# Written order for two engines only in the gate/up stage, and transform-D operands made as in the other blocks, in a Fourier-mixing and SwiGLU kernel on one Trainium2 core

## The chip, the cores and the metric

The kernel runs on one core of one Trainium2 chip, in float32. Its metric is the time of one execution in device microseconds. The engines of a core work side by side, each in the order of its own instruction queue: TensorE (PE; PEld is its weight load), ScalarE (ACT), VectorE (DVE), GpSimd (POOL) and SyncE (SP). SyncE issues nearly all transfers; GpSimd issues some, among them those that add to what lies in the destination (accumulating transfers).

## The reference

With x of 2048 x 512, w1 and w3 of 512 x 1376, w2 of 1376 x 512 and the real and imaginary parts of two discrete Fourier transforms:

```python
g = sigmoid((x * gate_w).sum(-1, keepdims=True))
a = x @ dft_hid_re.T
b = x @ dft_hid_im.T
y = dft_seq_re @ a - dft_seq_im @ b
h = silu(x @ w1) * (x @ w3)
out = g * y + (1 - g) * (h @ w2)
```

## The kernel before

**Products.** Each matrix product is done on 2 x 2 blocks with seven products instead of eight. Their operands are the blocks B11, B21 and B22 and the sums T1 = B12 + B11, T2 = T1 + B22, T3 = B22 + B12 and T4 = T2 + B21 (signs are put into the inputs on the host). Every operand is cut into a high and a low part: `split` (lines 110 and 111) makes the high part with a ScalarE copy and the low part with a VectorE subtraction. `mm3` (line 115) then issues three matmuls, high x high, high x low and low x high, so all TensorE work has line 115. The forms of the stationary side ("a1" and "a2", seven in all) are made by `forms1` (four of them, 1 MB) and `forms2` (three, 0.75 MB).

**Stages.** (1) *gate/up*: 22 items, one for each of 11 chunks of 128 columns of w1 and w3 and each half g of the tokens, with the exception that item 0 is done in a plain way ahead of the loop. (2) *F*: the transform along S, four blocks of 512 rows of the result; it comes before the transform along D here, and its result, scaled by g, goes to `zsp` in DRAM. (3) *H*: h @ w2, two blocks, with h read back from `hsp` and the result, scaled by 1 - g, stored to `nbsp`. (4) *Y*: the transform along D of z, two blocks, to which the `nbsp` part is added before it goes to `out`.

**gate/up.** `gate_up(n)` issues, for TensorE: X (six matmuls with form 4 of wb) and Z of item n, the first product X of item n + 3 (form 0 of its wa), X and Z of item n, Y of item n + 3, the last X of item n. That makes 42 matmuls; the last three items have no item n + 3 and 30 matmuls. An item's chunk comes as `ws` (load on SyncE, line 197); `prep_wa` splits three of its forms into `wa` (four buffers), `prep_wb` makes four sums on VectorE (lines 217 to 220) and splits them into `wb` (two buffers). The second time a chunk is used, `wb` is loaded from `wbsp` (line 202). ScalarE copies the first X and Z out of PSUM (lines 285 and 287) before TensorE may add to them again, applies silu (252 and 297), and VectorE adds and multiplies (250, 290, 292, 293, 298). GpSimd stores h (line 276). `extra[n]` holds more work, written after item n's own: the operands of the second token half (`sum_xo`, `split_xo`), the forms of part of w2 (`prep_w2`) and of x as stationary side of stage F (`make_a`). `prep_wa` for item n + 3 is written at the start of `gate_up(n)`, thus behind the extras of item n - 1.

**Order.** What is issued outside a region of written order is put in order by a planner with a timing model of its own; inside a region, each engine that the region names issues its instructions as they are written. In the kernel before, one region for all engines starts at `gate_up(1)` and ends with the kernel. What precedes it (loads, item 0, the first products of items 1 to 3) is ordered by the planner.

**Stages F, H and Y** run through one list, `STEPS`. A block has seven products in an order (`ORDER`), each in NQ steps: 4 in F, 3 in H, 2 in Y. A step issues 12 matmuls (6 for the last part of some H operands). The blocks begin at steps 0, 28, 56, 84 (F), 112, 133 (H), 154 and 168 (Y); the list ends at 182. `step(m)` issues the matmuls, then `advance(m)`: `load_c` loads operands whose entry in `LOADS` lies up to eight steps ahead, as far as the 13 buffers of 512 KB in `F4` are free; `sum_c` makes the T sum of step m + 4 on VectorE (line 532); `split_c` splits the operand of step m + 3 into one of four `zo` buffers. In F and H, T3 is made in the buffer of B22: after B22's split, GpSimd issues an accumulating transfer of B12 into it (line 548). In Y, T1 and T3 have loads of their own: SyncE loads B12 (line 557) and GpSimd adds B11 or B22 with an accumulating transfer (line 559).

The chain's order is P1 (B11), P5 (T1), P6 (T2), P3 (B22), P7 (T3), P2 (B21), P4 (T4). P1, P5, P6 and P3 use the first four forms, the others the last three. Both Y blocks of the kernel before use P1, P2, P5, P6, P3, P7, P4.

`at(block, n, f)` has f issued ahead of step n of a block. `load_forms` (line 691, on SyncE) loads a pair p of forms of the D matrices from `dsp`: the first four forms of p (1 MB) into buffer a1_k, the last three (0.75 MB) into a2_k, with k = 6, 7, 0, 1 for p = 0 to 3. Stage H uses buffers 0 to 5. `spill` (lines 647 to 659) scales or adds a result and stores it from SyncE. `close` at the end of gate/up gives the memory of its pools to stages F to Y.

The sites of the change are in the text below with their lines.

Of the kernel before, what the change touches and what calls it, by code (L numbers as in the profile page):

```python
# [10 lines left out]
ALU = mybir.AluOpType  # L11
# [4 lines left out]
F = 1376  # L16
KD = D // P
TB = 512
NTB = S // TB
NT = TB // P  # L20
NST = S // P
NG = NST // 2
NC = (F + P - 1) // P
NP2 = (NC + 1) // 2
# [9 lines left out]
def fnet_swiglu_gate_kernel(  # L34
# [20 lines left out]
    nc = tc.nc  # L55

    def pool(name, bufs, side, space=None):
        kw = {} if space is None else {"space": space}
        cm = tc.tile_pool(name=name, bufs=bufs, side=side, reuse_waits="tile", **kw)
        return cm, cm.__enter__()  # L60
# [37 lines left out]
    def wide(name):  # L98
        return take(F4, [P, 1024], F32, name)

    def parts(name):
        return take(ZO, [P, 2, 4, 256], F32R, name)

    def free(*tiles):
        for t in tiles:
            _, places, at = HELD.pop(id(t))
            places.append(at)

    def split(hi, lo, src):
        nc.scalar.activation(hi, src, AF.Copy)  # L110
        nc.vector.tensor_sub(lo, src, hi.bitcast(F32))  # L111
# [10 lines left out]
    dsp = [dram.tile([KD, P, 2, n, 256], F32, tag=f"dsp{n}", name=f"dsp{n}") for n in (4, 3)]  # L122
# [340 lines left out]
    for p, n in enumerate(A1_AT):  # L463
        extra.setdefault(n - 1, []).append(lambda p=p: load_a(p))
        extra.setdefault(n, []).insert(0, lambda p=p: make_a(p))
    extra.setdefault(NI - 2, []).append(lambda: load_a(NG - 1))
    extra[NI - 1] = [lambda: load_c(2)]


# [5 lines left out]
    CHAIN = (("P1", "B11"), ("P5", "T1"), ("P6", "T2"), ("P3", "B22"),  # L475
             ("P7", "T3"), ("P2", "B21"), ("P4", "T4"))

    NB = NTB + 4
    KIND = "F" * NTB + "HHYY"
    ORDER = [CHAIN] * (NTB + 2) + [tuple(CHAIN[i] for i in (0, 5, 1, 2, 3, 4, 6))] * 2  # L480
    NQ = [{"F": NG // 2, "H": NP2 // 2, "Y": KD // 2}[k] for k in KIND]
    STEPS = [(blk, q, k, form) for blk, nq in enumerate(NQ) for k, form in ORDER[blk]
             for q in range(nq)]
    START = [sum(NQ[:blk]) * len(CHAIN) for blk in range(NB + 1)]

    NEED = {
# [3 lines left out]
    }  # L490
    PLACE = {k: {"T1": "B12", "T2": "B12", "T4": "B12", "T3": "B22"} for k in "FH"}
    PLACE["Y"] = {"T2": "T1", "T4": "T1"}

    DONE = {k: ({"T1": "B11", "T4": "B21"}, {"T4": "B12", "T3": "B22"}) for k in "FH"}
    DONE["Y"] = {"T4": "B21"}, {"B11": "B11", "T4": "T1", "B22": "B22", "T3": "T3"}
    LEAD = 3
    AHEAD = 5
    RESULT = {"P3": 2, "P7": 3, "P2": 0, "P4": 1}
    FORM = {"P1": 0, "P5": 1, "P6": 2, "P3": 3, "P2": 0, "P4": 1, "P7": 2}
    RAW, ZT = {}, {}  # L500
    LOADS = sorted((START[blk] + n * nq - e * (blk > 0 or n != 1) + q, blk, k, q)
                   for blk, nq in enumerate(NQ) for q in range(nq) for k, n, e in NEED[KIND[blk]])

    def z_rows(tb, k):
        return zsp[(tb * 4 + k) * P : (tb * 4 + k + 1) * P, :]

    def block(blk, k, q):
        if KIND[blk] == "F":
            return cc[blk, ("B11", "B12", "B22", "B21").index(k), q]
        if KIND[blk] == "H":  # L510
            return hsp[blk - NTB, ("B11", "B12", "B21", "B22").index(k), q]
        return z_rows(2 * (blk - NTB - 2) + (k in ("B12", "B22")), 2 * (k in ("B21", "B22")) + q)

    def cols(blk, q, form):

        return 512 if KIND[blk] == "H" and q == NQ[blk] - 1 and form in ("B21", "B22", "T4") else 1024

    def done(m, j):
        blk, q, k, form = STEPS[m]
        if form in DONE[KIND[blk]][j]:  # L520
            free(RAW.pop((blk, DONE[KIND[blk]][j][form], q)))

    def sum_c(m):

        if not 0 <= m < len(STEPS):
            return
        blk, q, k, form = STEPS[m]
        b = {"T1": "B11", "T2": "B22", "T4": "B21"}.get(form)
        if b and form in PLACE[KIND[blk]]:
            n = cols(blk, q, b)  # L530
            t = RAW[blk, PLACE[KIND[blk]][form], q][:, :n]
            nc.vector.tensor_add(t, t, RAW[blk, b, q][:, :n])  # L532
        done(m, 0)

    def split_c(m):

        if not 0 <= m < len(STEPS):
            return
        blk, q, k, form = STEPS[m]
        src = RAW[blk, PLACE[KIND[blk]].get(form, form), q]  # L540
        ZT[m] = parts(f"zo{m}")
        t = ZT[m].rearrange("p h a n -> p h (a n)")
        n = cols(blk, q, form)
        split(t[:, 0, :n], t[:, 1, :n], src[:, :n])
        if form == "B22" and KIND[blk] != "Y":
            if n < 1024:
                nc.gpsimd.memset(src[:, n:], 0.0)
            nc.gpsimd.dma_start(src, block(blk, "B12", q), accum_op=ALU.add)
        done(m, 1)

    def load_c(m):

        while LOADS and LOADS[0][0] <= m and F4:
            _, blk, k, q = LOADS.pop(0)
            r = RAW[blk, k, q] = wide(f"{k}_{blk}_{q}")
            n = cols(blk, q, k)
            nc.sync.dma_start(r[:, :n], block(blk, "B12" if k in ("T1", "T3") else k, q)[:, :n])
            if k in ("T1", "T3"):
                nc.gpsimd.dma_start(r, block(blk, "B11" if k == "T1" else "B22", q),
                                    accum_op=ALU.add)  # L560

    def advance(m):
        load_c(m + LEAD + AHEAD)
        sum_c(m + LEAD + 1)
        split_c(m + LEAD)

    ctx.enter_context(tc.manual_schedule())
    for n in range(1, NI):
        gate_up(n)
        if ITEMS[n] == (NC - 1, 1):  # L570
            close(xo0_cm)
            a1_cm, a1 = pool("a1", 1, "left")

    split_c(0)
    split_c(1)
    close(*gate_pools)
    zo_b_cm, zo_b = pool("zo_b", 1, "right")
# [181 lines left out]
    def at(blk, n, f, *a):  # L759
        todo.setdefault(START[blk] + n, []).append((f, a))  # L760
# [10 lines left out]
    for i, (src, sp, p) in enumerate(late):  # L771
        blk, n = 1 + i // 2, 1 + i % 2 * 10
# [7 lines left out]
        at(NTB, p + 1, load_forms, "H", 1, p, w2sp, p)  # L780
    nh = 3 * NQ[NTB]
    for p in range(KD):
        at(NTB + 2, p - nh, load_forms, "Y", 0, p, dsp, (NP2 + p) % NG)
        at(NTB + 2, (p - 6, -2)[p >= NG - NP2], load_forms, "Y", 1, p, dsp, (NP2 + p) % NG)
    for blk in (NTB + 2, NTB + 3):
        for i, (k, form) in enumerate(ORDER[blk]):
            if k in RESULT:
# [66 lines left out]
```

## Time and profile before

| | |
|---|---|
| three runs, median | 819.0 us (817.43 to 820.0) |
| profiled execution | 816.77 us, span 815.0 us, mean granted clock 0.958 |
| TensorE busy | 751.5 us (92%), 3089 matmuls |
| VectorE, ScalarE busy | 576.3 us (71%), 365.4 us (45%) |
| GpSimd busy | 55.8 us (7%) |
| HBM | 132.64 MB read, 57.16 MB written, 233 GB/s |
| stages by the start of their matmuls | gate/up 5.6 us (24.3 for the loop), F 289.8, H 608.5, Y 717.0 |

TensorE's busy time is modelled, and a busy matmul can be one at a lower granted clock, so the count of matmuls in a stretch says more than its busy share: in stages F and H, 20 us hold 87 to 89 matmuls (0.225 us each).

### The profile page before, as it was taken

The page shows a single profiled execution, that of the slowest core. Times are in us where ns is not written, and L with a number is a line of the kernel's source. Part 1 is how long each engine was busy: PE and PEld are TensorE (multiplying, and loading weights), DVE is VectorE, ACT ScalarE, POOL GpSimd, SP SyncE. Part 2 cuts the span into 40 slices and gives each one's busy share as a digit, 9 for nine tenths or more (in the row PEclk, how much of TensorE's full clock was granted, in tenths as well). Part 3 has the DMA queues.
Part 4 walks back from the last instruction along what each step waited for, and adds up shares of the span by engine and source line. Part 5 has one row for each costly group of instructions (what it writes and reads, how often), then busy time and mean ns, then how long its engine had stood idle before and what let it go on. Part 6 is the DMA issues. An engine that isn't in the chain of part 4 may idle for free.

```text
span 815.0 us, 8527 instructions
## 1 busy us (share of the span) xinstructions
PE 751.5 (92%) x3089; PEld 594.1 (73%) x3089; DVE 576.3 (71%) x711; ACT 365.4 (45%) x485; POOL 55.8 (7%) x80
## 2 busy tenths in 40 slices
PE   9999888977868789999999999999999999977998
PEld 6777657765646567878878887888778778855886
DVE  7877766544455579698769877985878595844875
ACT  6554444333233346554545454444535445423452
POOL 0111000110000100100010010001000001000000
PEclk9999999888879879999999999999999999997999
DMA  6675323566365594858495658765999696797982
GB/s 232 202 303 192 142 90 116 188 218 226 137 241 205 219 399 181 227 213 317 144 286 209 243 171 242 279 237 162 316 397 402 167 312 151 257 385 241 347 266 79
DMA packets 50778, 190.36 MB, mean 234 GB/s; under 512 B 5296, under 2 KB 5424, under 8 KB 46128
## 3 DMA queue, kind: packets, MB, share of 16 engines
q1 hardware_dynamic: 40016, 144.20, 48.3%
q0 software_dynamic: 10432, 45.10, 19.3%
q8 instruction: 24, 0.39, 0.2%
q10 hardware_dynamic: 288, 0.52, 0.2%
q14 instruction: 18, 0.15, 0.1%
HBM read 132.64 MB, written 57.16 MB: 233 GB/s over the span
## 4 chain that ended last, share of the span: by engine, by line
PE 47%; DVE 18%; DMA 13%; issue 12%; ACT 9%; SPq 1%; POOL 0%; ACTq 0%; POOLq 0%; DVEq 0%
PE P L115 31%; PE X L115 9%; DMA B<-cc 5%; PE Z L115 4%; DVE zo L111 4%; ACT zo L110 3%; DMA B<-zsp 2%; DMA Y<-dsp 2%; DMA xs<-xn 1%; PE C L115 1%; DVE s L250 1%; DVE B L532 1%; DVE wa L111 1%; DMA B<-hsp 1%; DVE h L292 1%
## 5 line engine op out<-in xcount | busy, mean ns | idle before, releaser
L115 PE MATMUL P<-zo,a 128*128 128x512 f32 x1344 | 314.9, 395 | 5.6 <-DVE zo L111 3.8
L115 PEld LDWEIGHTS P<-zo,a 128*128 128x128 f32 x1344 | 253.5, 189 | 67.0 <-DVE zo L111 7.7
L111 DVE TENSOR_TENSOR zo<-B,zo 128x1024 fp32r<-128x1024 f32 (+1 forms) x166 | 197.6, 1201 | 89.4 <-ACT zo L110 88.8
L110 ACT ACTIVATE zo<-B 128x1024 fp32r<-128x1024 f32 (+1 forms) x166 | 171.3, 1041 | 190.4 <-PE P L115 69.3
L115 PE MATMUL X<-xo,wb 128*128 128x512 f32 x378 | 105.3, 427 | 9.1 <-ACT h L285 8.2
L115 PE MATMUL P<-zo,H 128*128 128x512 f32 x468 | 108.2, 392 | 0.4 <-DVE zo L111 0.4
L115 PEld LDWEIGHTS P<-zo,H 128*128 128x128 f32 x468 | 87.7, 188 | 20.8 <-DVE zo L111 1.3
L115 PEld LDWEIGHTS X<-xo,wb 128*128 128x128 f32 x378 | 78.2, 209 | 30.5 <-ACT h L285 10.3
L115 PE MATMUL P<-zo,Y 128*128 128x512 f32 x336 | 82.4, 407 | 11.8 <-DMA Y<-dsp 11.5
L115 PEld LDWEIGHTS P<-zo,Y 128*128 128x128 f32 x336 | 65.4, 196 | 28.7 <-DMA Y<-dsp 6.8
L532 DVE TENSOR_TENSOR B<-B,B 128x1024 f32<-128x1024 f32 (+1 forms) x66 | 78.1, 1183 | 0.2 <-DMA B<-hsp 0.2
L115 PE MATMUL X<-xo,wa 128*128 128x512 f32 x126 | 43.5, 473 | 31.6 <-ACT wa L110 26.9
L115 PEld LDWEIGHTS X<-xo,wa 128*128 128x128 f32 x126 | 24.9, 215 | 45.7 <-ACT wa L110 30.7
L252 ACT ACTIVATE s<-s 128x512 f32<-128x512 f32 x21 | 13.3, 631 | 70.0 <-DVE s L250 70.0
L290 DVE TENSOR_TENSOR u<-u,X 128x512 f32<-128x512 f32 x21 | 14.4, 684 | 38.2 <-PE X L115 38.1
L115 PE MATMUL Z<-xo,wa 128*128 128x512 f32 x126 | 34.9, 415 | 0.0
L298 DVE TENSOR_TENSOR h<-h,u 128x512 f32<-128x512 f32 x21 | 14.5, 692 | 26.6 <-ACT h L297 26.6
L115 PE MATMUL Y<-xo,wa 128*128 128x512 f32 x126 | 32.6, 393 | 0.0
L115 PE MATMUL Z<-xo,wb 128*128 128x512 f32 x126 | 32.5, 392 | 0.0
L115 PEld LDWEIGHTS Z<-xo,wa 128*128 128x128 f32 x126 | 26.3, 208 | 6.6
L276 POOL DMA_DIRECT2D hsp<-h x22 | 16.2, 736 | 181.4 <-DVE h L298 137.8
L115 PEld LDWEIGHTS Y<-xo,wa 128*128 128x128 f32 x126 | 23.7, 188 | 5.5
(109 smaller groups left out, 591.0 us busy)
## 6 DMA issues: line engine op xcount, KB each, us to landing
B<-cc SPq DMA_DIRECT2D x64, 512.0 KB, 6.5
hsp<-h POOLq DMA_DIRECT2D x22, 512.0 KB, 4.2
B<-hsp SPq DMA_DIRECT2D x20, 512.0 KB, 8.8
wbsp<-wb POOLq DMA_DIRECT2D x8, 1024.0 KB, 5.9
wb<-wbsp SPq DMA_DIRECT2D x8, 1024.0 KB, 5.1
B<-cc POOLq DMA_DIRECT2D x16, 512.0 KB, 10.2
H<-w2sp SPq DMA_DIRECT2D x6, 1024.0 KB, 9.8
B<-zsp SPq DMA_DIRECT2D x12, 512.0 KB, 13.0
```

Of the source, the lines that this page charges most:

```text
L110: nc.scalar.activation(hi, src, AF.Copy)
L111: nc.vector.tensor_sub(lo, src, hi.bitcast(F32))
L115: nc.tensor.matmul(ps, u, v, start=first and n == 0, stop=last and n == 2, skip_group_check=chain)
L250: nc.vector.tensor_add(s1, s1, y)
L252: nc.scalar.activation(s1, s1, AF.Silu)
L276: nc.gpsimd.dma_start(o.rearrange("b p n -> p b n"), h.rearrange("p (b n) -> p b n", b=2))
L290: nc.vector.tensor_add(u4, u4, x)
L292: nc.vector.tensor_add(u2, u2, z)
L298: nc.vector.tensor_mul(g1, g1, u4)
L532: nc.vector.tensor_add(t, t, RAW[blk, b, q][:, :n])
```

## The change

Three things are changed; what is computed stays the same. First, the region of written order around the gate/up loop names only TensorE and SyncE, so ScalarE, VectorE and GpSimd are ordered by the planner there. After the loop a region for all engines begins, as before. Second, in stage Y the first block takes the chain's order and only the last keeps the other. T1 and T3 of Y have no loads of their own any more: T1 is B12 plus B11 by a VectorE add, T3 is B22 plus an accumulating transfer of B12 after B22's split, as in F and H. Third, the loads of D forms are placed anew: pairs 0 and 1 at 24 and 23 (first forms) and 21 and 20 (last forms) steps ahead of stage Y, which is from three steps ahead of the second H block on. Pairs 2 and 3 come 7 and 6 steps ahead (first forms, as before) and one step ahead of and at the first step (last forms). Before, the first forms came 9 to 6 steps ahead and the last ones 6, 5, 2 and 2.

```diff
-    ORDER = [CHAIN] * (NTB + 2) + [tuple(CHAIN[i] for i in (0, 5, 1, 2, 3, 4, 6))] * 2
+    ORDER = [CHAIN] * (NB - 1) + [tuple(CHAIN[i] for i in (0, 5, 1, 2, 3, 4, 6))]
...
-    NEED = {
-        "F": (("B11", 0, 0), ("B12", 1, 1), ("B22", 2, 1), ("B21", 5, 0)),
-        "H": (("B11", 0, 0), ("B12", 1, 1), ("B22", 2, 1), ("B21", 5, 0)),
-        "Y": (("B11", 0, 0), ("B21", 1, 0), ("T1", 2, 6), ("B22", 3, 1), ("T3", 5, 6)),
-    }
-    PLACE = {k: {"T1": "B12", "T2": "B12", "T4": "B12", "T3": "B22"} for k in "FH"}
-    PLACE["Y"] = {"T2": "T1", "T4": "T1"}
-
-    DONE = {k: ({"T1": "B11", "T4": "B21"}, {"T4": "B12", "T3": "B22"}) for k in "FH"}
-    DONE["Y"] = {"T4": "B21"}, {"B11": "B11", "T4": "T1", "B22": "B22", "T3": "T3"}
+    NEED = [(("B11", 0, 0), ("B12", 1, 1), ("B22", 2, 1), ("B21", 5, 0))] * (NB - 1)
+    NEED.append((("B11", 0, 0), ("B21", 1, 0), ("B12", 2, 1), ("B22", 3, 1)))
+    PLACE = {"T1": "B12", "T2": "B12", "T4": "B12", "T3": "B22"}
+
+    DONE = {"T1": "B11", "T4": "B21"}, {"T4": "B12", "T3": "B22"}
...
-        if form == "B22" and KIND[blk] != "Y":
+        if form == "B22":
             if n < 1024:
                 nc.gpsimd.memset(src[:, n:], 0.0)
             nc.gpsimd.dma_start(src, block(blk, "B12", q), accum_op=ALU.add)
...
-            nc.sync.dma_start(r[:, :n], block(blk, "B12" if k in ("T1", "T3") else k, q)[:, :n])
-            if k in ("T1", "T3"):
-                nc.gpsimd.dma_start(r, block(blk, "B11" if k == "T1" else "B22", q),
-                                    accum_op=ALU.add)
+            nc.sync.dma_start(r[:, :n], block(blk, k, q)[:, :n])
...
-    ctx.enter_context(tc.manual_schedule())
+    order = tc.manual_schedule(engines={mybir.EngineType.PE, mybir.EngineType.SP})
+    order.__enter__()
     for n in range(1, NI):
         gate_up(n)
         if ITEMS[n] == (NC - 1, 1):
             close(xo0_cm)
             a1_cm, a1 = pool("a1", 1, "left")
 
+    order.__exit__(None, None, None)
+    ctx.enter_context(tc.manual_schedule())
     split_c(0)
     split_c(1)
     close(*gate_pools)
...
     for p in range(KD):
-        at(NTB + 2, p - nh, load_forms, "Y", 0, p, dsp, (NP2 + p) % NG)
-        at(NTB + 2, (p - 6, -2)[p >= NG - NP2], load_forms, "Y", 1, p, dsp, (NP2 + p) % NG)
+        early = p < NG - NP2
+        at(NTB + 2, p - (24 if early else nh), load_forms, "Y", 0, p, dsp, (NP2 + p) % NG)
+        at(NTB + 2, p - (21 if early else 3), load_forms, "Y", 1, p, dsp, (NP2 + p) % NG)
```

The rest of the diff replaces look-ups by kind of block by the single tables above.

More of the change, by code (lines that the diff above doesn't have):

```diff
@@ L501, in fnet_swiglu_gate_kernel @@
     LOADS = sorted((START[blk] + n * nq - e * (blk > 0 or n != 1) + q, blk, k, q)
-                   for blk, nq in enumerate(NQ) for q in range(nq) for k, n, e in NEED[KIND[blk]])
+                   for blk, nq in enumerate(NQ) for q in range(nq) for k, n, e in NEED[blk])
     def z_rows(tb, k):
@@ L519, in done @@
         blk, q, k, form = STEPS[m]
-        if form in DONE[KIND[blk]][j]:
-            free(RAW.pop((blk, DONE[KIND[blk]][j][form], q)))
+        if form in DONE[j]:
+            free(RAW.pop((blk, DONE[j][form], q)))
     def sum_c(m):
@@ L528, in sum_c @@
         b = {"T1": "B11", "T2": "B22", "T4": "B21"}.get(form)
-        if b and form in PLACE[KIND[blk]]:
+        if b:
             n = cols(blk, q, b)
-            t = RAW[blk, PLACE[KIND[blk]][form], q][:, :n]
+            t = RAW[blk, PLACE[form], q][:, :n]
             nc.vector.tensor_add(t, t, RAW[blk, b, q][:, :n])
@@ L539, in split_c @@
         blk, q, k, form = STEPS[m]
-        src = RAW[blk, PLACE[KIND[blk]].get(form, form), q]
+        src = RAW[blk, PLACE.get(form, form), q]
         ZT[m] = parts(f"zo{m}")
```

## The prediction, made before the changed kernel was built or run

> **What bounds the kernel now.** I read the forty slices first. TensorE shows 9 in nearly all slices from 320 to 700 us; it falls off in slices 5 to 15 (about 100 to 310 us, gate/up) and in slice 36 (720 to 740 us, the start of the D transform). The time to be won lies there. Next, windows cut at the start of each gate/up item (time range, length, busy us of PE, PEld, DVE, ACT and POOL, granted clock, DMA share, GB/s), with one window at the D start:
>
> ```profile
> 45.93:55.73 9.80, 9.80 (x44) 7.90 (x43) 7.17 (x12) 4.60 (x7) 1.28 (x2) 1.00 0.73 293
> 136.57:153.05 16.48, 12.74 (x43) 9.57 (x42) 8.40 (x15) 5.51 (x10) 1.97 (x3) 0.79 0.54 199
> 180.17:194.18 14.01, 11.72 (x43) 8.89 (x42) 6.80 (x12) 4.62 (x8) 0.72 (x1) 0.88 0.51 178
> 136.57:286.33 149.76, 118.52 (x428) 90.66 (x427) 77.67 (x132) 51.74 (x91) 14.09 (x21) 0.85 0.56 202
> 717.00:741.00 24.00, 12.16 (x41) 8.37 (x39) 8.37 (x8) 7.22 (x8) 1.71 (x2) 0.79 1.04 381
> ```
>
> The same 42 matmuls take 9.80 us where nothing is missing and 14.0 to 16.5 us where chunk or token preparation stands between. No engine is full in the long ones: VectorE has 6.80 us of work in 14.01. So this is an order problem, not a load problem. The waits between 23 and 300 us name the instructions:
>
> ```profile
> ACT s L252 <- DVE s L250: 70.0, 18, 5.8
> PEld X L115 <- ACT wa L110: 30.7, 9, 7.5
> PEld X L115 <- DVE wa L111: 11.0, 15, 1.2
> PEld X L115 <- ACT h L285: 10.3, 5, 3.8
> ```
>
> The timeline of the item at 180.17 shows how it comes about:
>
> ```profile
> 184.67 0.84 ACT L110 ACTIVATE a<-xm 128x768 fp32r<-128x768 f32 x1 [2.04 <-DVE xm L141]
> ...
> 185.42 0.83 ACT L110 ACTIVATE wa<-ws 128x768 fp32r<-128x768 f32 x1
> ...
> 186.30 0.73 PE L115 MATMUL X<-xo,wa 128*128 128x512 f32 x2 [1.89 <-ACT wa L110]
> ...
> 187.43 1.55 PE L115 MATMUL X<-xo,wa 128*128 128x512 f32 x4 [0.39 <-DVE wa L111]
> ```
>
> The split of wa needs only a loaded ws and the wa buffer that the Z product of the item before released, but ScalarE has it written behind the last silu of that item (L297) and behind make_a, whose second copy stands 2.04 us for VectorE's xm. Earlier in the item ScalarE idled up to 5.8 us at L252 with nothing allowed ahead. After such a gap the clock falls too.
>
> **Gate/up, the order of ScalarE, VectorE and GpSimd.** No instruction is added or removed. What is to be won is the excess over undisturbed items. Eight items from 35.89 to 126.91 take 91.0 us against 8 x 9.80 = 78.4, excess 12.6; nine to 255.84 take 128.9 against 9 x 9.66 (the item at 126.91) = 86.9, excess 42.0; the last three, of 30 matmuls (30 x 0.228 = 6.85), take 30.5 against 20.5, excess 9.9. Sum **64.5 us**. With ScalarE free to choose, the wa copy (0.83) and subtraction (0.96) fit in the 24 matmuls (5.5 us) between the Z product that frees the buffer and the first product that needs it.
> A bad order of the planner's is bounded by rows: 0 left over if every item runs like that at 45.93, and half, 32 us, if late splits remain in every second item. I take 0.65 us for each of 20 items, 13 us: the items at 55.73 and 66.29 took 10.56 and 10.61, 0.8 over, with a single 1.05 us xo split ahead of wa, at clock 1.00. The planner's own order can be read only ahead of gate_up(1): TensorE is busy 18.81 of the first 20 us with VectorE and ScalarE at 14. That speaks for the low half. **Gain 52 (32 to 64).**
> Cover for it: VectorE has 148 us of work between 35.89 and 286.33, and 186 would be left. DMA: 202 GB/s x 149.8 us = 30.2 MB in 98 us (8 x 9.66 + 20.5) is 309 GB/s, under the 381 of the last window above. SyncE's queue keeps its order, so loads start as soon as before relative to TensorE.
> What a gap costs beyond itself: the item at 180.17 waits 1.89 + 0.39 us and is 4.35 over 9.66, so 2.1 more went to the clock (0.88). The Trainium skill (TensorE: Matmul & The Clock Gate, "HAM oscillation — how this bites in real kernels") puts the danger at TensorE gaps over some 3.4 us. The trace here loses clock at 2.3 us. If ten such gaps stayed, the rule would price them at 10 x 2.3 = 23 us, the row at 10 x 4.35 = 43.
>
> **Gate/up to transform along S.** From 288.2 to 312.2 TensorE issues 73 matmuls (73 x 0.2247 = 16.4, from 89 in 20 us) in 24 us: 7.6 lost to the two first splits behind the last silu, and to an xs load that lands in 12 us at DMA share 0.99. The second region is written in full as before; only the splits may slip ahead of the last gate/up work. Bounds 0 and 6; I take **2**.
>
> **The D start, T1 and T3, early forms.** Between 717.0 and 750.2 TensorE issues some 72 matmuls, 16.2 us of work, in 33.2: **17 us lost**. The DMA engines are full from 701 to 741 (share 1.0, about 365 GB/s, 14.6 MB), and Y<-dsp has the last word:
>
> ```profile
> PE P L115 <- DMA Y<-dsp: 11.5, 3, 5.8
> ```
>
> Four edits empty this burst. (a) Two pairs of forms, 2 x (1 + 0.75) = 3.5 MB, leave it for the start of the second w2 h block (640 to 660 us: 171 GB/s, share 0.56). There they stand in SyncE's queue beside the B<-hsp loads, which lead their use by 8 steps, some 21 us; 3.5 MB at 365 GB/s is 10 us, so it is covered, and would cost up to 5 us without that lead. (b) T1 drops its accumulating transfer for a VectorE add: 4 x 1.22 us in all; VectorE is at 44.5 of 64 us after 751, hidden. T3 drops the second read of a block: both together save 2 MB per block. So 14.6 - 5.5 = 9.1 MB, 25 us, with the first steps' share in front. (c) The first Y block takes the chain's order: its second forms are needed at step 8 instead of step 2, some 16 us later. (d) T3 is now B22 plus an accumulating DMA that GpSimd can issue only after B22's split, two steps ahead of T3's. The w2 h block shows the price of the chain:
>
> ```profile
> 680.49 1.05 ACT L110 ACTIVATE zo<-B 128x1024 fp32r<-128x1024 f32 x1
> 681.57 1.23 DVE L111 TENSOR_TENSOR zo<-B,zo 128x1024 fp32r<-128x1024 f32 x1 [1.98 <-ACT zo L110]
> ...
> 683.20 0.85 POOL L548 DMA_DIRECT2D B<-hsp  x1 [49.66 <-DVE zo L111]
> ...
> 691.37 1.06 ACT L110 ACTIVATE zo<-B 128x1024 fp32r<-128x1024 f32 x1 [1.60 <-DMA B<-hsp]
> 692.46 1.23 DVE L111 TENSOR_TENSOR zo<-B,zo 128x1024 fp32r<-128x1024 f32 x1 [1.44 <-ACT zo L110]
> ```
>
> From the start of B22's split to the end of T3's it takes 13.2 us (680.49 to 693.69), for the second of the pair 14.3 (682.76 to 697.03). In Y there are five steps of 12 matmuls in between (three of lead, two between the forms): 13.5 us. So it just misses, by 0 to 1 us a block; landings of up to 12 instead of 8.2 us would make that 4. Queued behind T3's split on ScalarE are the next block's splits. I take 1 us a block, 2 in all (0 to 8), and 1 (0 to 5) for what is left of the start: **gain 14 (4 to 17).**
>
> **Sum:** 816.8 (profiled execution, span 815.0) - 52 - 2 - 14 = 748.8. The profiled execution lies 2.2 under the median of the three runs, so I forecast **751**. All best bounds give 732, all worst 783.
>
> **Rivals.**
> *Half of gate/up only*, 18%: the planner's view of when things are ready is not the chip's, and in every second item a wa split or an L285 copy comes late; or the compressed stage meets a DMA limit (30.2 MB at 250 GB/s is 121 us instead of 98, 23 us back). For it: wb loads land in 5.1 us at 170 to 250 GB/s and have one item, 9.6 us, to do so. Against it: the item at 35.89 ran at share 1.00 and 357 GB/s in 10.04 us. With some 29 of gate/up's us gained instead of 52: 751 + 23, about 774.
> *Gate/up unchanged*, 5%: the planner keeps emission order on the free engines, so the change does not do there what it says. Only the D start pays: 819 - 14 = 805. Against it: ahead of gate_up(1), where the planner orders all, two X matmuls of item 1 stand at 15.40 between C matmuls of item 0.
> *Slower*, 11%: the planner puts consumers of loads (wa from ws, a from xr) at the head of ScalarE's queue as if data were there at once. The real landings are 4.2 to 6.3 us for ws and 5.5 for xr; ScalarE would stand with L285 behind it, whose slack is the 12 matmuls (2.7 us) of Z and X less its own 0.6. A stand of 5.5 us is then a gap of 3.4, with the clock's 2 us 5.4 an item, 20 x 5.4 = 108 against today's 64.5: 819 + 43 - 16 = 846. It turns slower from 4.0 us of loss an item ((64.5 + 16) / 20). Against it: in the planner's stretch of before, ScalarE's waits for loads are 0.2 to 1.4 us each.
>
> **Numbers.** The forecast, 66%, has its own range 731 to 770. The range 728 to 795 adds the half gain and leaves out the unchanged gate/up, the slower case and a tail. Within 0.3% (2.5 us, about what a measurement of this kernel can tell from no change) gets 1%; faster 88%, slower 11%.
>
> **What would show it.** Right: items of 9.6 to 10.5 us with clock 1.00 between 36 and the start of P; PEld X <- ACT wa under 5 us in total; first P matmul near 237 us; the first Y step without a wait for Y<-dsp; T3 splits waiting some us on an accumulate while TensorE loses under 2. Wrong: ScalarE waiting for ws or xr with L285 behind it; waits of X for wb<-wbsp; a TensorE gap ahead of P7 in Y.

## The result and the profile after

| | before | after |
|---|---|---|
| median | 818.89 us (817.43 to 820.0, 4 runs) | 753.57 us (752.89 to 756.34, 4 runs) |
| profiled execution | 816.77 us, span 815.0 us | 754.2 us, span 752.4 us |
| mean granted clock | 0.958 | 0.993 |
| last matmul of gate/up ends | 288.2 | 233.6 |
| first matmul of F | 289.83 | 236.47 |
| first matmul of Y | 717.0 | 664.61 |
| from there to the end | 98.0 us | 87.8 us |

The ratio of the times is 0.921, with a 95% interval of 0.9181 to 0.9238: 65 us less. The last four rows say where. By the end of gate/up 54.6 us are won; 1.2 of them go before the first matmul of F and 1.0 during F and H; Y gives 10.2 more. Together 62.6, the difference of the two spans.

The head of the page of the changed kernel, with its forty slices:

```profile
span 752.4 us, 8533 instructions
PE 726.2 (97%) x3089; PEld 580.0 (77%) x3089; DVE 574.7 (76%) x715; ACT 367.0 (49%) x485; POOL 52.4 (7%) x76
...
PE   9999999989897899999999999999999999999996
...
PEclk9999999999999999999999999999999999999999
...
HBM read 128.45 MB, written 57.16 MB: 247 GB/s over the span
```

TensorE now has a 9 almost everywhere. The same 3089 matmuls take 726.2 us of modelled time instead of 751.5; the clock falls much less in gate/up (0.99 granted from 23 to 240 us). HBM reads are 4.19 MB fewer, the 2 MB that each Y block no longer reads a second time.

Windows cut at the starts of gate/up items, as before (time range, length, busy us of PE, PEld, DVE, ACT and POOL, granted clock, DMA share, GB/s):

```profile
145.12:156.43 11.31, 9.69 (x44) 7.70 (x42) 4.71 (x9) 4.24 (x7) 1.27 (x2) 1.00 0.61 221
185.91:195.43 9.52, 9.52 (x44) 7.88 (x42) 7.87 (x15) 3.96 (x8) 1.97 (x3) 1.00 0.87 285
195.43:209.54 14.11, 11.41 (x43) 8.98 (x42) 7.25 (x14) 4.88 (x9) 0.74 (x1) 0.88 0.67 272
```

Most items are like the one at 185.91: 9.52 us with TensorE busy throughout. Three of the 17 with 42 matmuls after 35.79 us stand out, with 11.43 us (at 45.99), 11.31 (at 145.12) and 14.11 (at 195.43). The waits of the loop, 23 to 240 us (engine, line, what it waited for: us in all, times, longest):

```profile
ACT s L252 <- DVE s L250: 20.1, 13, 4.6
...
DVE xm L139 <- DMA gs<-sc: 5.7, 1, 5.7
ACT wa L110 <- DMA ws<-w: 5.7, 1, 5.7
ACT zo L110 <- issue: 5.7, 1, 5.7
...
PEld X L115 <- DVE u L290: 4.5, 3, 2.0
...
PEld X L115 <- ACT h L297: 3.3, 2, 3.1
...
PEld X L115 <- DVE wa L111: 1.2, 1, 1.2
```

X no longer waits for wa copies (30.7 us before, none now), and its waits for wa subtractions fell from 11.0 to 1.2. In their place stand three waits of 5.7 us each, on ScalarE and VectorE. One of them in the timeline of ScalarE:

```profile
192.30 0.59 ACT L242 ACTIVATE s<-X 128x512 f32<-128x512 f32 x1
198.60 0.85 ACT L110 ACTIVATE wa<-ws 128x768 fp32r<-128x768 f32 x1 [5.71 <-DMA ws<-w]
200.90 0.42 ACT L110 ACTIVATE a<-xr 128x256 fp32r<-128x256 f32 x1 [1.45 <-DMA xr<-xn]
201.22 0.61 ACT L252 ACTIVATE s<-s 128x512 f32<-128x512 f32 x1
201.74 0.58 ACT L297 ACTIVATE h<-X 128x512 f32<-128x512 f32 x1
202.22 0.59 ACT L285 ACTIVATE h<-X 128x512 f32<-128x512 f32 x1
203.87 0.84 ACT L110 ACTIVATE a<-xm 128x768 fp32r<-128x768 f32 x1 [1.06 <-DVE xm L141]
```

and what TensorE makes of it and of the first split of F:

```profile
202.37 2.34 PE L115 MATMUL X<-xo,wa 128*128 128x512 f32 x6 [2.70 <-ACT h L297]
204.51 2.47 PE L115 MATMUL X<-xo,wb 128*128 128x512 f32 x6
206.81 1.53 PE L115 MATMUL Z<-xo,wa 128*128 128x512 f32 x6
...
236.47 0.50 PE L115 MATMUL P<-zo,a 128*128 128x512 f32 x1 [2.85 <-ACT zo L110]
```

The planner put the wa split and make_a's first copy (of xr) ahead of the silu (L297) of the item, but neither load had landed: ScalarE stood 5.71 us for ws and 1.45 us more for xr. The first product of a later item needs the bank of PSUM (the memory into which TensorE adds) that this silu reads, so TensorE stood 2.70 us; then 12 matmuls took 4.44 us (202.37 to 206.81) where 12 undisturbed ones take 2.72. The first split of F does the same: it stands 5.70 us at the head of ScalarE's queue with the last silu behind it. There the profile names no releaser ("issue"); the experiment with the w2 step, below, comes back to it.

In Y the first matmuls run without a wait for forms. The gap is now in the last block:

```profile
664.61 25.30 PE L115 MATMUL P<-zo,Y 128*128 128x512 f32 x109
690.11 42.21 PE L115 MATMUL P<-zo,Y 128*128 128x512 f32 x179 [0.20 <-DVE zo L111]
735.03 0.50 PE L115 MATMUL P<-zo,Y 128*128 128x512 f32 x1 [2.71 <-ACT zu L726]
735.80 12.57 PE L115 MATMUL P<-zo,Y 128*128 128x512 f32 x47 [0.27 <-DVE zo L111]
```

The gap at 735 is the first T3 product of the last block. The page names ScalarE's zu; zu, the copy of the earlier result out of PSUM, stood behind the T3 split on ScalarE, which waited for the accumulating transfer (shown further down). The 48 matmuls from there on ran at a clock of 0.87 and took some 2.0 us too long (13.07 us without the 0.27 gap, against 48 x 0.2313 = 11.10 by the 672 matmuls in 155.44 us of F).

Windows cut finely show what the clock does. It is granted at 0.50 from 203.10 to 206.51, from 237.23 to 240.64 and from 735.58 to 738.99, and at 1.00 from each of these stretches to the next. So it is halved for 3.41 us at a time, which costs some 1.7 us of work: once right after the 2.70 us gap, once at the gaps of F's first matmuls (2.85 and 0.76), once at those at 735 (2.71 and 0.27).

### The profile page after: what moved, and what is told of

The parts are those of the page before. It is cut to its first block, busy times and chain, and to the rows that moved or that the text cites. A ratio compares the mean times of both kernels' runs of the same rounds, so it can differ in the third digit from the quotient of the medians.

```text
span 752.4 us, 8533 instructions
## 1 busy us (share of the span) xinstructions
PE 726.2 (97%) x3089; PEld 580.0 (77%) x3089; DVE 574.7 (76%) x715; ACT 367.0 (49%) x485; POOL 52.4 (7%) x76
## 4 chain that ended last, share of the span: by engine, by line
PE 31%; issue 24%; DMA 21%; DVE 16%; ACT 6%; SPq 1%; POOL 1%; POOLq 0%; ACTq 0%; DVEq 0%
PE P L115 19%; DMA B<-cc 8%; PE X L115 7%; DVE zo L111 5%; ACT zo L110 4%; DMA B<-zsp 3%; DMA xr<-xn 3%; PE Z L115 3%; DVE B L527 2%; PE Y L115 2%; DMA B<-hsp 1%; DMA dsp<-late 1%; PE C L115 1%; DMA nb<-nbsp 1%; DMA gs<-sc 1%
## 5 line engine op out<-in xcount | busy, mean ns | idle before, releaser
L115 PEld LDWEIGHTS P<-zo,a 128*128 128x128 f32 x1344 | 252.2, 188 | 71.1 <-DVE zo L111 10.5
L110 ACT ACTIVATE zo<-B 128x1024 fp32r<-128x1024 f32 (+1 forms) x182 | 187.7, 1043 | 218.1 <-PE P L115 76.7
L111 DVE TENSOR_TENSOR zo<-B,zo 128x1024 fp32r<-128x1024 f32 (+1 forms) x182 | 216.9, 1203 | 98.1 <-ACT zo L110 97.4
L115 PE MATMUL X<-xo,wb 128*128 128x512 f32 x378 | 95.4, 396 | 4.2 <-DVE u L290 3.2
L527 DVE TENSOR_TENSOR B<-B,B 128x1024 f32<-128x1024 f32 (+1 forms) x78 | 92.8, 1190 | 2.5 <-DMA B<-hsp 2.4
L115 PEld LDWEIGHTS X<-xo,wb 128*128 128x128 f32 x378 | 71.4, 190 | 22.1 <-DVE u L290 4.5
L115 PE MATMUL X<-xo,wa 128*128 128x512 f32 x126 | 33.9, 401 | 3.5 <-ACT h L297 2.7
L290 DVE TENSOR_TENSOR u<-u,X 128x512 f32<-128x512 f32 x21 | 14.4, 684 | 20.3 <-PE X L115 20.0
L115 PEld LDWEIGHTS Z<-xo,wa 128*128 128x128 f32 x126 | 23.4, 188 | 7.1 <-ACT u L287 1.9
L115 PEld LDWEIGHTS Z<-xo,wb 128*128 128x128 f32 x126 | 23.6, 188 | 5.3
L543 POOL DMA_DIRECT2D B<-cc x16 | 13.7, 858 | 200.5 <-DVE zo L111 186.6
L110 ACT ACTIVATE wa<-ws 128x768 fp32r<-128x768 f32 (+2 forms) x21 | 17.0, 810 | 19.0 <-PE Z L115 11.8
## 6 DMA issues: line engine op xcount, KB each, us to landing
H<-w2sp SPq DMA_DIRECT2D x6, 1024.0 KB, 10.2
```

The source lines that it names most:

```text
L115: nc.tensor.matmul(ps, u, v, start=first and n == 0, stop=last and n == 2, skip_group_check=chain)
L290: nc.vector.tensor_add(u4, u4, x)
```

## Experiments

### The two parts apart

The kernel before, with only its gate/up region named for TensorE and SyncE:

```diff
-    ctx.enter_context(tc.manual_schedule())
+    order = tc.manual_schedule(engines={mybir.EngineType.PE, mybir.EngineType.SP})
+    order.__enter__()
     for n in range(1, NI):
...
+    order.__exit__(None, None, None)
+    ctx.enter_context(tc.manual_schedule())
```

> The kernel before with only the gate/up region changed: written order for TensorE and SyncE. If the two halves of the change are independent, it takes the gate/up part alone: the first P matmul comes near 236.5 us as in the changed kernel (289.8 before), and the time is 819 - 53 = 766 us, within 3. Rival: part of the gate/up gain needs the new D stage (or the D burst grows when it comes sooner): above 772.

Measured: 767.40 us, ratio 0.9373 (0.9342 to 0.9405), as expected for independent halves. First matmul of F at 237.43.

The changed kernel with all engines written in gate/up again:

> The changed kernel with the gate/up region in written order for all engines again. If the halves are independent: first P matmul near 290 us and stage Y 88 us long as in the changed kernel (98 before), 819 - 10 = 809 us, within 3. Rival: above 815, if the Y part only pays in the compressed kernel.

Measured: 806.62 us, 0.9865 (0.9824 to 0.9906). First matmul of F at 288.35. This too is within the 3 us that the expectation allowed. So the order is worth some 50 us and the Y part some 11, and the two hardly touch each other: 817.8 - 50.4 - 11.1 = 756.3, against 753.57 with both. The 2.7 us between them are no more than these intervals leave open.

### Which engine had to be free

The changed kernel, with only ScalarE left to the planner in gate/up:

```diff
-    order = tc.manual_schedule(engines={mybir.EngineType.PE, mybir.EngineType.SP})
+    order = tc.manual_schedule(engines={mybir.EngineType.PE, mybir.EngineType.SP,
+                                        mybir.EngineType.DVE, mybir.EngineType.Pool})
```

> The changed kernel with VectorE and GpSimd in written order too in gate/up, so that only ScalarE is the planner's. Theory A, as the prediction has it (ScalarE's written order holds the wa split back): at least 40 of the 54 us of gate/up stay won, 768 us or less. Theory B (VectorE's written order holds it back as well, since wa's subtraction stands behind L298 and the extras' subtractions, whatever ScalarE does): at most 20 stay won, 788 us or more, and the X matmuls wait for DVE wa instead of ACT wa.

Measured: 807.05 us, 0.9865 (0.983 to 0.9899). That is what the Y part gives by itself: freeing ScalarE alone won nothing in the whole time. In the two traces it brings the first matmul of F forward by 4.2 us (284.19 against 288.35), but the 74th begins at 310.25 against 310.67: the start of F takes the gain back. The timeline of this run shows why:

```profile
177.24 0.85 ACT L110 ACTIVATE wa<-ws 128x768 fp32r<-128x768 f32 x1 [1.11 <-PE Z L115]
...
181.23 0.42 DVE L111 TENSOR_TENSOR a<-xr,a 128x256 fp32r<-128x256 f32 x1
...
184.07 0.96 DVE L111 TENSOR_TENSOR a<-xm,a 128x768 fp32r<-128x768 f32 x1 [1.17 <-ACT a L110]
184.95 0.95 DVE L111 TENSOR_TENSOR wa<-ws,wa 128x768 fp32r<-128x768 f32 x1
...
185.95 1.56 PE L115 MATMUL X<-xo,wa 128*128 128x512 f32 x4 [2.83 <-DVE wa L111]
```

ScalarE now copies wa as soon as Z frees the buffer (177.24). But the low part is VectorE's, and VectorE's written order has the whole of make_a ahead of it; it starts at 184.95, 6.9 us after the copy is done. X waits there 40.6 us in all, 15 times.

The mirror image, with VectorE free and ScalarE written:

```diff
+    order = tc.manual_schedule(engines={mybir.EngineType.PE, mybir.EngineType.SP,
+                                        mybir.EngineType.Activation, mybir.EngineType.Pool})
```

> The changed kernel with ScalarE and GpSimd in written order too in gate/up, so that only VectorE is the planner's. Theory A: the wa copy stays behind L297 and the extras' copies, little is won, 790 us or more. Theory B: with VectorE free the xm and T sums are ready early, ScalarE's extras run without their waits of 2 us and more, and only the copies themselves (0.4 to 2.3 us an item) stand ahead of wa: most stays won, 758 to 775 us.

Measured: 776.97 us, 0.9492 (0.9453 to 0.9532), first matmul of F at 257.73. That is 2 us above the range that theory B named and far from A's. VectorE's freedom by itself brings some 30 us (806.62 to 776.97); the other 23 need ScalarE as well. What was left:

```profile
PEld X L115 <- DVE wa L111: 18.2, 14, 5.7
PEld X L115 <- ACT wa L110: 12.3, 11, 3.2
```

And GpSimd, written in order in the changed kernel:

```diff
+    order = tc.manual_schedule(engines={mybir.EngineType.PE, mybir.EngineType.SP, mybir.EngineType.Pool})
```

> The changed kernel with GpSimd written in order in gate/up too (TensorE, SyncE and GpSimd written, VectorE and ScalarE free). Theory 'only the freedom of VectorE and ScalarE counts': 752 to 755 us, as the changed kernel. Rival 'GpSimd's share matters, since it issues accumulating transfers in the first w2 steps': over 757 us.

Measured: 754.78 us, 0.9237 (0.9223 to 0.9252), as the changed kernel. GpSimd's order is of no account.

### Can the written order do it by a move

If a late wa split were the whole matter, writing it earlier should do as well as the planner. All engines written; the split moved between the Z product that frees its buffer and the next first product (the first such split, for item 4, goes ahead of the loop):

```diff
         def b1():
+            if n + LOOK < last and WSET[n + LOOK + 1] not in WA:
+                prep_wa(WSET[n + LOOK + 1])
             if n + LOOK <= last:
...
-        if n + LOOK <= last and WSET[n + LOOK] not in WA:
-            prep_wa(WSET[n + LOOK])
         second(n, (b0, b1))
```

> Written order for all engines in gate/up, as in the run with the D part alone (806.6 us), but the wa split of item n + 4 is written into item n right behind its Z product, ahead of the silu, the last X and the extras, on ScalarE and VectorE at once. If the gate/up loss is the place of the wa split: the waits of X for wa go from 42 us of weight-load idle to under 5, what is left is L285 behind the extras (the last three items keep their 9.9 us, the items with part of w2 some 4 each), 26 of 64 us lost, so 764 to 775 us. Rival, that the planner gains by many small moves and not by this one: 781 us or more.

Measured: 788.33 us, 0.9648 (0.9622 to 0.9675): 18 of some 53 us. The theory of the place falls. The wa waits are gone (1.2 us), but the next work in the line waits instead:

```profile
PEld X L115 <- ACT h L285: 35.3, 14, 6.7
```

```profile
212.52 0.40 ACT L110 ACTIVATE w2a<-w2r 128x256 fp32r<-128x256 f32 x1
215.23 0.84 ACT L110 ACTIVATE w2a<-w2m 128x768 fp32r<-128x768 f32 x1 [2.31 <-DVE w2m L141]
...
217.75 0.58 ACT L285 ACTIVATE h<-X 128x512 f32<-128x512 f32 x1
...
218.38 2.93 PE L115 MATMUL X<-xo,wb 128*128 128x512 f32 x6 [6.23 <-ACT h L285]
```

The extras (make_a, prep_w2) still stand in one piece between two items, and the copy of X out of PSUM (L285) is behind them. The last step was to write the extras earlier too, behind that split:

```diff
         def b1():
+            if n + LOOK < last and WSET[n + LOOK + 1] not in WA:
+                prep_wa(WSET[n + LOOK + 1])
+            for f in extra.get(n, ()):
+                f()
...
-        for f in extra.get(n, ()):
-            f()
```

> As the run with the wa split moved by hand, and the extras of item n too are written behind that split, ahead of Y and the last X of the item, where ScalarE and VectorE idled. If place is all, a written order does what the planner's does: 750 to 760 us. Rival: extras written there delay L290 and L285, more than 768 us.

Measured: 803.35 us, 0.9823 (0.9804 to 0.9843), nearly all lost again. That is the rival's number, though the wait is for L297 and hardly for L285 (6.5 us):

```profile
PEld X L115 <- ACT h L297: 38.9, 12, 7.3
```

Now the extras stand ahead of L250, L252 and the silu L297. Three written places of the same work give three different last waits: wa, L285, L297. The explanation that fits all of this is that each item has only short free stretches on ScalarE and VectorE, and that the extras fit when they are cut up over them. The planner does cut them up: in the timeline of ScalarE after the change, above, make_a's two copies (200.90 and 203.87) have L252, L297 and L285 between them. None of these three orders does so. A written order with the extras cut up was not run, so this last step is argued and not shown.

### Y: bytes and chain

The changed kernel with the form loads of pairs 0 and 1 at their old steps:

```diff
-        early = p < NG - NP2
-        at(NTB + 2, p - (24 if early else nh), load_forms, "Y", 0, p, dsp, (NP2 + p) % NG)
-        at(NTB + 2, p - (21 if early else 3), load_forms, "Y", 1, p, dsp, (NP2 + p) % NG)
+        at(NTB + 2, p - nh, load_forms, "Y", 0, p, dsp, (NP2 + p) % NG)
+        at(NTB + 2, (p - 6, -2)[p >= NG - NP2], load_forms, "Y", 1, p, dsp, (NP2 + p) % NG)
```

> The changed kernel with the D forms loaded where they were before (9 to 6, and 6, 5, 2 and 2 steps ahead). If the 3.5 MB moved out of the burst are what removes the stall at the D start: 758 us or more, with TensorE waiting for Y<-dsp or for B<-zsp at the first steps. Rival: the chain's order in the first Y block and the 2 MB saved suffice, since the last forms are needed six steps later: within 2 us of the changed kernel's 753.6.

Measured: 760.33 us, 0.9295 (0.9271 to 0.932), as the theory of the bytes has it. The other way round, the kernel with the order alone plus the early loads, with T1, T3 and the order of the products as before:

> The kernel with the planner's gate/up and the Y stage of before (767.4 us), with only the loads of pairs 0 and 1 moved 24 and 21 steps ahead. If the burst's bytes set the stall (14.6 MB less 3.5): 3.5 MB at 365 GB/s is 9.6 us, so 757 to 761 us. Rival: order decides, because P2 as second product needs pairs 2 and 3 of the last forms, which still come two steps ahead: 763 us or more, with TensorE still waiting for Y<-dsp.

Measured: 759.87 us, 0.9289 (0.9265 to 0.9312). The time is that of the theory, but the wait that the rival named is there too:

```profile
679.98 1.62 PE L115 MATMUL P<-zo,Y 128*128 128x512 f32 x3 [5.46 <-DMA Y<-dsp]
683.27 71.19 PE L115 MATMUL P<-zo,Y 128*128 128x512 f32 x297 [1.67 <-DMA Y<-dsp]
```

Stage Y from its first matmul to the end, by the four traces:

| | old T1, T3, order | new T1, T3, order |
|---|---|---|
| old loads | 100.2 us | 93.6 us |
| early loads | 93.2 us | 87.8 us |

Each half brings some 6 us, with or without the other. The two waits for forms that the early loads alone leave are gone only with the second half.

### The residues

The last Y block, with product P2 put between B22 and T3:

```diff
-    ORDER = [CHAIN] * (NB - 1) + [tuple(CHAIN[i] for i in (0, 5, 1, 2, 3, 4, 6))]
+    ORDER = [CHAIN] * (NB - 1) + [tuple(CHAIN[i] for i in (0, 1, 2, 3, 5, 4, 6))]
...
-    NEED.append((("B11", 0, 0), ("B21", 1, 0), ("B12", 2, 1), ("B22", 3, 1)))
+    NEED.append((("B11", 0, 0), ("B12", 1, 1), ("B22", 2, 1), ("B21", 4, 0)))
```

> The changed kernel with the last Y block's products in the order 0,1,2,3,5,4,6 instead of 0,5,1,2,3,4,6, so that one product (24 matmuls' worth of TensorE work per half) lies between the last load of the T3 chain's partner and the T3 product. Theory 'the T3 chain in the last block is the mis-sized term': the gap of 2.71 us at 735.03 and the slow matmuls behind it (2.2 us) go, 749 us (748 to 751). Rival 'the accumulate into B lands whenever the transfers allow and the wait only moves to another product or to the tail': 753 to 755 us, with a TensorE gap over 2 us somewhere else behind 715.

Measured: 751.06 us, 0.9185 (0.9162 to 0.9208), just above the range that was expected, and 3.7 under the kernel with GpSimd written, which ran beside it; the intervals of these two lie apart. TensorE's last stretch:

```profile
713.42 30.39 PE L115 MATMUL P<-zo,Y 128*128 128x512 f32 x131 [0.48 <-DVE zo L111]
```

131 matmuls without a gap; stage Y takes 83.9 us instead of 87.8. So the accumulate's wait, with the clock behind it, cost 3.9 us.

On top of it, the fourth early step of w2 two items earlier:

```diff
-W2_AT = (10, 12, 16, 20)
+W2_AT = (10, 12, 16, 18)
```

> As e10_last_block_order, with the fourth early w2 step of gate/up placed at 18 instead of 20, so that the buffers that it reads come free two items earlier and the loads that the first transform behind gate/up waits for are issued earlier. Theory 'the 2.85 us before the first P product is a late load': that gap falls under 1 us and the wait of ScalarE's first zo split (5.7 us) goes, 2 to 4 us under e10_last_block_order, 745 to 748 us if that one is 749. Rival 'the planner sets that split behind something else, or the extra transfers delay the items': within 1.5 us of e10_last_block_order or slower.

Measured: 747.94 us, 0.9161 (0.9137 to 0.9185). The medians are 3.1 apart, though the intervals overlap; the trace shows the gap gone, with the first F product now amid the last item of gate/up:

```profile
229.81 0.49 PE L115 MATMUL P<-zo,a 128*128 128x512 f32 x1 [0.47 <-ACT zo L110]
```

The gain came, but not for the reason that the expectation gave. The first loads of B for F are issued no earlier (219.96 us, against 218.79 in the changed kernel). What the split had stood for is the buffer that it writes: w2a and w2b of the early w2 steps are taken from the same `zo` buffers. These are the store of w2a and the split in the changed kernel's timeline, and the store's row among its transfers between 216 and 242 us (KB, us from issue to landing):

```profile
223.24 0.58 POOL L443 DMA_DIRECT2D w2sp<-w2a  x1 [0.16 <-issue]
235.36 2.00 ACT L110 ACTIVATE zo<-B 128x1024 fp32r<-128x1024 f32 x2 [5.70 <-issue]
```

```profile
w2sp<-w2a POOLq DMA_DIRECT2D x1, 1024.0 KB, 12.0
```

Issued at 223.24 and 12.0 us long, the store ends at 235.24, and the split starts at 235.36. Two items earlier the store is issued at 209.98 and is long done.

Last, the load of ws written ahead of the wb load, which stands for a buffer that TensorE still reads:

```diff
         def b0():
-            w = WSET[min(n + LOOK, last)] + 1
-            if w < len(SETS) and w not in WA and w not in WS:
-                load_w(w, 0, 3 if back(w) else 4)
...
+        w = WSET[min(n + LOOK, last)] + 1
+        if w < len(SETS) and w not in WA and w not in WS:
+            load_w(w, 0, 3 if back(w) else 4)
         if n < last and WSET[n + 1] not in WB and back(WSET[n + 1]):
             load_wb(WSET[n + 1])
```

> As e11_last_block_and_w2, with the load of ws put in SyncE's written order ahead of the load of wb of the same item (which stands for a buffer that TensorE still reads) instead of behind it. Theory 'the gap left in gate/up near 200 us is ScalarE standing for a ws load that is issued late': ScalarE's wait of 5.70 us for ws goes, with it TensorE's gap of 3.56 us at 203.38 and the slow matmuls behind it, 4 to 5 us under e11_last_block_and_w2, 742 to 745 us. Rival 'the load is late because the transfers are full, or the planner finds another place to stand': within 1.5 us of e11_last_block_and_w2, with a gap of over 2 us somewhere between 180 and 230.

Measured: 745.04 us, 0.9116 (0.9088 to 0.9144), at the edge of the theory's range. The wait for ws is gone, but ScalarE stands at nearly the same time for another load, so the rival is partly right:

```profile
197.07 0.42 ACT L110 ACTIVATE w2a<-w2r 128x256 fp32r<-128x256 f32 x1 [5.31 <-DMA w2r<-w]
...
200.82 1.66 PE L115 MATMUL X<-xo,wa 128*128 128x512 f32 x6 [1.92 <-ACT h L297]
```

The gap is 1.92 us instead of 3.56 and costs no clock any more. The medians of this step are 2.9 us apart, its intervals just touch; but against the changed kernel (0.9181 to 0.9238) the interval lies wholly below, so this version beats both kernels.

## Why the prediction held, point by point

**The total: close, and in part because errors offset.** By the profiled executions gate/up gives 54.6 us where 52 were forecast, its end a loss of 1.2 where a gain of 2 was, and Y 10.2 where 14 were; F and H, which the sum left out, take 1.0 longer. That makes 62.6 instead of 68. The medians lie 65.3 apart, since the profiled execution of before lies 2.1 under its median and that of after 0.6 over its own. So 751 came within 2.6 us of 753.57 partly by luck. Two of the signs that the prediction named for its being wrong did show, each once: ScalarE standing for ws, and a gap ahead of P7 in Y.

**Gate/up: right in size, with an incomplete reason.** 52 us were forecast, and the last gate/up matmul ends 54.6 us earlier. The sum of the excess over undisturbed items (64.5 us) was the right measure, and 10.5 of it are left by the same sum (the items from 35.79 to 232.10 take 196.3 us against 185.8). But the working said that with ScalarE free to choose, the copy and the subtraction of wa fit in the 24 matmuls. The experiment with ScalarE alone free gained nothing, and the one with VectorE alone free gained 30. The view of waits named ScalarE's copy (30.7 us) because VectorE's subtraction, stuck behind the same make_a, ended only a little later (11.0): a wait for two things shows the rest of the second, not its whole lateness.

**The residue: near in sum, wrong in form.** I took 0.65 us for each of 20 items, 13 in all. Instead most items lose nothing and a few lose much: gaps of 1.35, 1.62, 2.70, 0.42 and 0.99 us and 1.7 us of lower clock make 8.8 of the 10.5. Of these, the 2.70 and the 1.62 are the rival "slower", in small: an instruction put at the head of its queue as if the transfer that it needs were done (wa for the load of ws; xm for a buffer that the store of the gate scores, gs, still read; 5.7 us each). The readers of PSUM behind them were L297 and L290, not the L285 that the rival named. The rival priced such a stand at 5.4 us; at 195.43 it cost 4.45 (14.11 less 9.66). It missed by its frequency: twice in the loop, not 20 times.

**Gate/up to F: wrong sign.** Forecast a gain of 2; it is a loss of 1.2 by the first F matmul, and the 73 matmuls for which the prediction counted 24.0 us from the end of gate/up now take 25.4 (233.62 to 259.00). The bounds (0 and 6) held no loss, because the splits were thought free to slip ahead of the last gate/up work, but not to stand there. The split of F stood 5.70 us ahead of the last silu, for a buffer that a late store still read. Moving that store's w2 step removed the gap.

**D start: 10.2 instead of 14, and one term was mis-sized.** The step is the T3 chain, "1 us a block, 2 in all". In the first block it cost 0.20 us at TensorE, and ScalarE waited 6.90 us, as foreseen. In the last it cost 3.9. These lines of VectorE, SyncE, GpSimd and ScalarE around it say what was late:

```profile
718.60 1.28 DVE L730 TENSOR_TENSOR zs<-zs,P 128x512 f32<-128x512 f32 x2
719.91 1.23 DVE L648 TENSOR_TENSOR zs<-zs,nb 128x1024 f32<-128x1024 f32 x1
721.06 3.49 DVE L111 TENSOR_TENSOR zo<-B,zo 128x1024 fp32r<-128x1024 f32 x3
...
721.61 1.98 SPq L674 DMA_DIRECT2D nb<-nbsp  x3
...
723.81 0.85 POOL L543 DMA_DIRECT2D B<-zsp  x1 [43.91 <-DVE zo L111]
...
733.43 1.06 ACT L110 ACTIVATE zo<-B 128x1024 fp32r<-128x1024 f32 x1 [10.60 <-DMA B<-zsp]
```

B22's first copy is the second of a pair that starts at 717.66, so it begins near 718.6; T3's subtraction ends near 735.7. That is 17 us instead of the 13.2 taken from the w2 h block, against a cover of 13.5. VectorE was busy 23.90 of the 24.54 us before 714.65 and had the sums of the results (L730, L648) ahead of B22's subtraction, so the accumulate was issued late, and it took 9.6 us from issue to ScalarE's start instead of 8.2. I had called VectorE's adds hidden from its average over 64 us. By these lines the accumulate is issued 5.2 us after B22's copy begins instead of 2.7, so of the 3.9 us that the chain is longer 2.5 are the late issue and some 1.5 the longer transfer. The transfer had company: SyncE had issued three loads of nb, 512 KB each, from 721.61 on, and the DMA share was 0.99 from 723.81 to 733.43. In the run with the last block reordered the same three loads are issued at 711.37, the accumulates at 718.59 and 720.32, and these land within 5.2 and 6.0 us. So the reordering gave the chain more time and also took the loads out of its way; which of the two would have been enough was not separated. In that run, with the chain out of the way, stage Y gains 14.1 us (98.0 to 83.9), which is the forecast's figure.

**Early forms: covered, as said.** With the order alone Y begins at 665.78 us without them and at 666.07 with them, so the 3.5 MB cost nearly nothing in the w2 h block (0.6 us from the first matmul of F on), and by the table above they bring 5.8 to 7.0 us of Y.

**The clock.** The Trainium skill (TensorE: Matmul & The Clock Gate, "HAM oscillation — how this bites in real kernels") puts the danger at gaps over some 3.4 us. These traces differ: the gap of 2.70 us cost 1.7 us in the 12 matmuls behind it and that of 2.71 (and 0.27) in Y some 2.0, while after 1.62 us (156.43) and 1.92 us (the last experiment, 200.82) the next matmuls ran at full rate. What decides whether a gap brings the 3.41 us at half clock is not shown here. In the run with VectorE free, two gaps of 1.27 and 0.51 us with two matmuls between them cost clock as well: the six matmuls at 160.15 took 2.71 us instead of 1.52.

## What to carry to other kernels

Where a written order leaves gaps and no engine is full, free every engine that a late operand passes through, not the one that the waits name: freeing one alone can be worth nothing. Here a planner that cut the side work up over short free stretches did better than each of three written places, but it also put work at the head of a queue whose load had not landed, or whose buffer a store still held. So look afterwards for stands of several us with a PSUM reader behind them, and issue those transfers earlier. Price a chain through a transfer where it stands, with the queue of each engine at that moment, and with the loads in flight beside it, not by an average share over a longer stretch.

## What was not expected of the hardware

A gap of less than 3 us can cost nearly as much again in clock: 2.70 + 1.7 us in gate/up and 2.98 + 2.0 in Y, while gaps of 1.62 and 1.92 cost only themselves. In the changed kernel each loss is one stretch of 3.41 us at a granted clock of 0.50. Accumulating transfers fill the DMA engines at a low rate: from 720.40 to 725.60 in the run with the last block reordered, two of 512 KB and nothing else move, and the DMA share is 1.01 at 184 GB/s; from 711.40 to 719.50, with mostly plain loads, it is 0.99 at 344 GB/s. There these transfers landed in 5.2 and 6.0 us; beside three loads of 512 KB, in the changed kernel, it was 9.6 us from the issue to the start of the split that waited.
